# A sparse attention with two feed-forward stages: the product with v in 64x64 tiles, its halves added in DRAM, the last keys' transposes in spare PSUM columns

## The chip, the cores and the metric

One core of one Trainium2 chip runs the whole program. The metric is the device time of one execution in microseconds; the core is the only one, so it is also the slowest. TensorE, VectorE, ScalarE, GpSimd and SyncE run side by side, each through its own instructions in order; TensorE accumulates in PSUM, eight banks of 512 float32 columns on 128 partitions, and DMA queues move data to and from DRAM.

## The reference, cut to what matters

```python
def _attn_ref(q, k, v, tau):             # (4, 8, 576, 64) each
    scores = scale * np.matmul(q, k.transpose(0, 1, 3, 2))
    thresh = np.max(scores, axis=-1, keepdims=True) - tau
    scores = np.where(scores >= thresh, scores, -1000000000.0)
    attn = np.exp(scores - np.max(scores, axis=-1, keepdims=True))
    attn = attn / (np.sum(attn, axis=-1, keepdims=True) + 1e-09)
    return np.matmul(attn, v)

x = attn_out.transpose(0, 2, 1, 3).reshape(2304, 512)
x = ((x @ w_a) * (x @ w_b)) @ w_out      # 512 -> 1536 -> 512
h = x @ w_in                             # 512 -> 1024
solu = h * softmax(h)
out = layernorm(solu) * g_ln @ w_out     # 1024 -> 512
```

All arrays are float32. The change touches the first part, attention, alone.

## The kernel before, in words

**Pairs and steps.** The 32 heads are handled as 16 pairs of two heads (index `i` or `j`). A pair has 576 queries and keys a head; they are cut into nine score blocks (`NS` = 9, index `s`): blocks 0 to 7 are 128 queries of one head, block 8 the last 64 queries of both heads. The loop over `m` takes two blocks a step, "A" and "B", so 72 steps hold the scores of all pairs and six more steps drain what follows. Two pairs take nine steps, so the work of step `m` repeats with `m` mod 9. `PROG` lists, by letters, the order in which a step emits its parts, and that order is each engine's order.

**One step.** `scores` (A, B) multiplies q and k in four 64x64 tiles of the array into a two-bank PSUM tile `ps`, 288 of the 512 columns of each bank; the pool has two such tiles, one for A and one for B. `soft_max` (VectorE, line 692) negates and scales them into SBUF and takes the row minimum; `soft_exp` (ScalarE, line 704) takes the exponentials; `soft_thr` (t, u; GpSimd, line 709) makes the threshold; `soft_mask` (a, b; VectorE, line 718) applies it and sums the row. One step later `tpose` (T, U; line 738) transposes the masked blocks on TensorE into a PSUM tile `tp`, four 128-column transposes a block, and ScalarE copies them to SBUF (line 731). The 64 last keys of two blocks (`tq`, line 754) and those of block 8 (line 757, a product with the identity) go through `tpose_tail` (Y) into another tile of the same three-buffer pool.

**The product with v.** `pv` (V; line 769) has one accumulation for 256 queries (`r` = 1) and one for 320 queries and two columns of ones (`r` = 2): 128 keys a product for `kc` 0 to 3, two heads in the two column halves of the array (128x64 tiles), and for `kc` = 4 the last 64 keys of the two heads, with zeros in the other head's rows of `vz`. The dictionary `PV` spreads these over the steps: pair `j` begins at step `j*9//2 + 4`, two or three `kc` a step. ScalarE then copies `po` to `xp` (line 777), and SP stores `xp` to the DRAM tensor `xd` in the next step (line 779). `finish` (F) transposes the reciprocal row sums and stores them to `rzd`.

**Beside it.** In steps 6 to 41 `conv_emit` slips in the preparation of the next stage's weights in a fixed order: at most one VectorE operation in `fill` (letter f, ahead of the masks) and up to three ScalarE or GpSimd operations at the step's end. GpSimd's are tensor_tensor operations of 256 or 512 elements (line 237), and `gate` makes them wait for the step's last mask. At step 46 the program loads `rzd` and `xd` of the first third of the tokens (`load_z(0)`, `load_x(0)`), and from step 51 a list `STEPS` hands out their normalisation and splitting, at steps 65 and 66 `load_z(1)` and `load_x(1)`; from step 69 VectorE normalises the second third (line 483). After the loop `load_x(2)` loads the last third (line 470), and the second stage, `moe1`, begins; its weight loads `wraw` (line 200) follow on SP's queue, which works in order. `bank["y"]` are four PSUM tiles that take the place of the score tiles from step 72.

Of the kernel before, what the change touches and what calls it, by code (L numbers as in the profile page):

```python
# [21 lines left out]
def kernel(  # L22
# [607 lines left out]
    def attention():  # L630
        es, es_r = ExitStack(), ExitStack()
        slots, late, bulk = [], [], []
        conv_ops = conv_first()
        ps_a = es.enter_context(tc.tile_pool(name="ps_a", bufs=3, space=PSUM))
# [10 lines left out]
        dt = {}  # L645
        for k in (0, 1, "t"):
            for r in (1, 2):
                shape = [P] + ([] if k == "t" else [NQ]) + [R1 if r == 1 else R2 + 2]
                dt[k, r] = d = pt.tile(shape, F32, name=f"pt{k}{r}")
                if r == 2:  # L650
                    nc.vector.memset(d[(slice(None),) * (len(shape) - 1) + (slice(R2, R2 + 2),)], 1.0)
        vz = [pt.tile([P, 2, D], F32, name=f"vz{k}") for k in range(3)]
        for z in vz:
            nc.gpsimd.memset(z, 0.0)
# [78 lines left out]
        def tpose(i, s):  # L733
            pe = st[i, s]
# [11 lines left out]

        def tpose_tail(i, s):
            pe = st.pop((i, s))
            if s == 3 or s == 2 * NQ:
                r, q0, n = (1, 0, R1) if s == 3 else (2, 2, R2)  # L750
# [9 lines left out]
        def pv(i, r, half):  # L760
            n = R1 if r == 1 else R2 + 2
            if half == 0:
                st[i, "o", r] = ps_a.tile([P, 512], F32, name="po", bufs=1)
            po = st[i, "o", r][:, 0:n]
            vr, vt = ld[i, "v"], vz[i % 3]

            def mm(kc, h):
                lhsT, rhs = (vr[:, h * NQ + kc], dt[h, r][:, kc, 0:n]) if kc < NQ else (vt[:, h], dt["t", r][:, 0:n])
                nc.tensor.matmul(po[h * D:(h + 1) * D], lhsT=lhsT, rhs=rhs, start=(kc == 0), stop=(kc == NQ), skip_group_check=True)  # L769

            def store():
                b, hp = divmod(i, NPAIR)
                if r == 1:
                    st[i, "x"] = px.tile([P, S + 2], F32, name="xp")
# [6 lines left out]
            if half == 1:  # L781
                pv_q.append(store)
            cut = NQ // 2
            return [lambda kc=kc, h=h: mm(kc, h) for kc in (range(cut) if half == 0 else range(cut, NQ + 1)) for h in range(2)]

        def finish(i):
            b, hp = divmod(i, NPAIR)
            rz = st.pop((i, "rz"))
            t1 = ps_a.tile([P, 512], F32, name="rt1", tag="tp")
            nc.tensor.transpose(t1[0:NS, 0:P], rz, ident)  # L790
            zt = sm.tile([NS, P], F32, name="zt", bufs=2)
            zd = rzd[b][2 * hp:2 * hp + 2]

            def store():
                nc.scalar.activation(out=zt, in_=t1[0:NS, 0:P], func=AF.Copy)
# [5 lines left out]
        PV = [{x: (k // 2 + 1, k % 2) for k, x in enumerate(d)} for d in ([4, 5, 6, 7], [4, 5, 7, 8])]  # L801
# [41 lines left out]
        PROG = 'ABtuVFTUYXfab'  # L843
# [5 lines left out]
        for m in range(tot // 2 + 6):  # L849
# [43 lines left out]
            for ch in PROG:  # L893
                if ch in "AB":
                    score("AB".index(ch))
                elif ch == "V":
                    for mm in mms:
                        mm()
                elif ch == "F":
                    for j in range(NP):  # L900
                        if m - j * NS // 2 == 8:
                            finish(j)
                elif ch in "TU":
                    turn("TU".index(ch))
                elif ch == "Y":
                    for c in old:
                        tpose_tail(*c)
# [27 lines left out]
            bulk.clear()  # L935
            for fn in dma_q + later:
# [17 lines left out]
            if m in conv_at:  # L954
                conv_emit("AP", 3)
# [15 lines left out]
        for fn in dma_q + later:  # L971
# [526 lines left out]
```

## Time and profile before

| | us |
|---|---|
| median of 3 runs | 902.83 |
| lowest and highest of them | 902.67 and 903.42 |
| the profiled execution | 902.6 |
| its span, first to last instruction | 900.8 |
| steps 9 to 71 of attention, in the profile | from 35.73 to about 264 |

The profiled execution's own time is 1.8 us more than its span, and 0.2 us under the median. TensorE's granted clock is full in the whole span. A busy TensorE is not one at its peak, so the starts of its weight loads are read below, and waits are read where the engine in question sat idle.

### The profile page before, as it was taken

How to read it: one execution, taken by the hardware profiler on the slowest of the kernel's cores; microseconds unless marked ns; L12 is line 12 of the kernel's file. 1: busy time of each engine (PE TensorE's matmuls, PEld its weight loads, DVE VectorE, ACT ScalarE, POOL GpSimd, SP SyncE). 2: the span in 40 equal slices, each digit the busy share in tenths (PEclk: the TensorE clock that was granted, in tenths of full speed). 3: DMA queues.
4: the chain of work that ended last, by engine and by line, in shares of the span. 5: the costliest groups of instructions: out<-in, count | busy, mean ns of one | idle time of the engine just before them, and what ended most of it. 6: DMA issues, size and time to landing. Idle time of an engine off the chain costs nothing.

```text
span 900.8 us, 16285 instructions
## 1 busy us (share of the span) xinstructions
PE 881.3 (98%) x5842; PEld 732.7 (81%) x5842; DVE 690.3 (77%) x1508; ACT 530.3 (59%) x1010; POOL 161.7 (18%) x296
## 2 busy tenths in 40 slices
PE   7999999999989999999999999999999999999998
PEld 3555555555558899999999999999999778888886
DVE  6989988899988877876586655775544898888873
ACT  5888877878965465554454444544445465555543
POOL 1143321124412010002121121211113000000000
PEclk9999999999999999999999999999999999999999
DMA  6435334566555869489965998588869011110001
GB/s 176 155 112 150 117 106 126 133 175 212 167 188 175 252 241 313 139 313 314 354 117 115 317 337 230 104 216 268 255 138 213 25 43 52 47 47 24 24 25 47
DMA packets 71280, 147.71 MB, mean 164 GB/s; under 512 B 11040, under 2 KB 41376, under 8 KB 71200
## 3 DMA queue, kind: packets, MB, share of 16 engines
q1 hardware_dynamic: 60032, 131.84, 43.7%
q0 software_dynamic: 10368, 14.16, 10.8%
q8 instruction: 46, 0.75, 0.3%
q10 hardware_dynamic: 800, 0.68, 0.3%
q14 instruction: 34, 0.28, 0.1%
HBM read 98.06 MB, written 48.59 MB: 163 GB/s over the span
## 4 chain that ended last, share of the span: by engine, by line
PE 82%; DVE 9%; issue 3%; ACT 2%; DMA 2%; POOL 1%; ACTq 0%; SPq 0%; DVEq 0%; POOLq 0%
PE acc L611 28%; PE py L1098 16%; PE po L1392 10%; PE ph L1271 9%; PE po L769 5%; PE ps L687 5%; PE tp L738 5%; DVE pe L718 3%; DVE ns L692 3%; PE pl L1369 2%; POOL st_t L237 1%; PE py L611 1%; ACT pe L704 1%; DMA rzd<-zt 1%; DMA q<-in_qkv_dram 1%
## 5 line engine op out<-in xcount | busy, mean ns | idle before, releaser
L611 PE MATMUL acc<-xt,w 128*128 128x384 f32 x1446 | 270.6, 336 | 2.6 <-DVE xt L237 2.6
L611 PEld LDWEIGHTS acc<-xt,w 128*128 128x128 f32 x1446 | 254.4, 188 | 3.6 <-DVE xt L237 3.6
L704 ACT ACTIVATE pe<-ns,nm 128x576 f32<-128x576 f32 x128 | 94.0, 775 | 47.7 <-DVE ns L692 47.0
L1076 POOL DMA_DIRECT2D yd<-y x68 | 59.0, 891 | 305.2 <-ACT y L1072 209.4
L692 DVE TENSOR_SCALAR_CACHE_REDUCE ns<-ps 128x576 f32<-128x576 f32 x144 | 103.1, 752 | 8.9 <-PE ps L687 8.6
L718 DVE SCALAR_TENSOR_TENSOR pe<-ns,th,pe 128x576 f32<-128x576 f32 x128 | 100.2, 813 | 6.2 <-ACT pe L704 3.8
L1392 PE MATMUL po<-w,lt 128*128 128x512 f32 x432 | 103.5, 395 | 0.0
L687 PE MATMUL ps<-k,q 64*64 64x288 f32 x1152 | 90.1, 424 | 5.2 <-DMA k<-in_qkv_dram 3.6
L1392 PEld LDWEIGHTS po<-w,lt 128*128 128x128 f32 x432 | 79.8, 188 | 16.8
L1072 ACT ACTIVATE y<-py 128x384 f32<-128x384 f32 x92 | 45.0, 490 | 75.9 <-PE py L1098 73.9
L1098 PE MATMUL py<-ga,wo 128*128 128x384 f32 x432 | 84.0, 334 | 0.0
L1098 PE MATMUL py<-gb,wo 128*128 128x384 f32 x432 | 84.0, 334 | 0.0
L769 PE MATMUL po<-pt,vr 128*64 128x322 f32 (+1 forms) x512 | 77.6, 419 | 1.5 <-ACT pt L731 1.1
L731 ACT ACTIVATE pt<-tp 128x512 f32<-128x512 f32 (+1 forms) x160 | 77.9, 544 | 1.6 <-PE tp L738 0.8
L738 PEld LDWEIGHTS tp<-ident,pe 128*128 128x128 f32 x512 | 56.5, 143 | 26.0 <-issue 9.9
L709 POOL TENSOR_SCALAR th<-nm,toff 128x1 f32<-128x1 f32 x144 | 47.4, 331 | 158.7 <-DVE ns L692 153.1
L1098 PEld LDWEIGHTS py<-ga,wo 128*128 128x128 f32 x432 | 75.7, 188 | 0.0
L1098 PEld LDWEIGHTS py<-gb,wo 128*128 128x128 f32 x432 | 75.7, 188 | 0.0
L1271 PE MATMUL ph<-w,ys 128*128 128x512 f32 x297 | 74.5, 393 | 0.7 <-ACT h L1275 0.7
L738 PE MATMUL tp<-ident,pe 128*128 128x128 f32 x512 | 71.8, 280 | 2.4 <-DVE pe L718 1.2
L1271 PEld LDWEIGHTS ph<-w,ys 128*128 128x128 f32 x297 | 55.6, 188 | 13.7 <-ACT h L1275 1.1
L769 PEld LDWEIGHTS po<-pt,vr 128*64 128x64 f32 x512 | 32.0, 136 | 42.5 <-issue 17.1
(148 smaller groups left out, 1186.5 us busy)
## 6 DMA issues: line engine op xcount, KB each, us to landing
xt<-opd SPq DMA_DIRECT2D x42, 768.0 KB
wraw<-in_w_dram SPq DMA_DIRECT2D x36, 512.0 KB
opd<-xt SPq DMA_DIRECT2D x21, 768.0 KB
yd<-y POOLq DMA_DIRECT2D x68, 192.0 KB, 5.3
q<-in_qkv_dram SPq DMA_DIRECT2D x15, 576.0 KB
k<-in_qkv_dram SPq DMA_DIRECT2D x30, 176.0 KB
xd<-xp SPq DMA_DIRECT2D x16, 289.0 KB
yd<-y SPq DMA_DIRECT2D x24, 192.0 KB
```

The costliest lines, as they stand in the source:

```text
L611: nc.tensor.matmul(ps, lhsT=w[:, WOP[j], wi, c * P:(c + 1) * P], rhs=x[:, c, xi, :], start=(k == 0 and j < 3), stop=(k == 3 * QK - 1 and j ...
L687: nc.tensor.matmul(ps[t * D:(t + 1) * D, g, 0:HS], lhsT=q[r, u, c], rhs=k[r, u, o:o + HS], start=True, stop=True, skip_group_check=True)
L692: nc.vector.tensor_scalar(out=ns, in0=st[i, s][:, :, 0:HS], scalar1=-SCALE, scalar2=None, op0=ALU.mult, op1=ALU.min, accum_out=nm)
L704: nc.scalar.activation(out=pe.rearrange("p (g s) -> p g s", g=2), in_=ns, func=AF.Exp, bias=nm, scale=-1.0)
L718: last_mask[0] = nc.vector.scalar_tensor_tensor(out=pv, in0=ns, scalar=th, in1=pv, op0=ALU.is_le, op1=ALU.mult, accum_out=z[:, s:s + 1])
L731: evac_q.append(lambda: nc.scalar.activation(out=out, in_=in_, func=AF.Copy))
L738: nc.tensor.transpose(tp[:, kc, :], pe[:, o:o + P], ident)
L769: nc.tensor.matmul(po[h * D:(h + 1) * D], lhsT=lhsT, rhs=rhs, start=(kc == 0), stop=(kc == NQ), skip_group_check=True)
L1076: nc.gpsimd.dma_start(out=to[:, g["oc"], :], in_=y, accum_op=ALU.add)
L1098: nc.tensor.matmul(g["py"], lhsT=wos[g["q"] * F1 + r][:, wi, oc * P:(oc + 1) * P], rhs=g["g"][r][:, gi, :], start=(r == c == 0), stop=last ...
L1271: nc.tensor.matmul(ps, lhsT=v[:, a, c * P:(c + 1) * P], rhs=w[:, b], start=(k == 0 and j < 3), stop=(k == 3 * QK - 1 and j in (2, 4, 6)), ...
L1392: nc.tensor.matmul(po, lhsT=lt[:, a, j, :], rhs=w2(j, b), start=(k == 0), stop=(k == 3 * NJ - 1))
```

## The change

`pv` works in 64x64 tiles: each product over 128 keys becomes two over 64 keys, in the two row halves of the array, and each row half has a PSUM bank of its own. `po` takes two banks and its pool `tp` has two buffers in place of three. The last keys need no zeros, so `vz` with its fills and loads goes. ScalarE copies both banks to `xp`, SP stores the first half, and GpSimd adds the second half to it in DRAM by an accumulating DMA, two steps after the copy was emitted. `load_x` reads what was added up. The products of `PV` are spread anew. The last keys' transposes, and that of the row sums, go to the columns of the A block's score tile that hold no scores (from step 72 into `bank["y"][3]`); block 8's, in 64x64 tiles, directly behind the product with v (`tail_end`). They are copied out by ScalarE at the new letter E, that is behind the step's two exponentials. `conv_emit` emits at most some 512 elements of GpSimd's operations a step.

```diff
-        ps_a = es.enter_context(tc.tile_pool(name="ps_a", bufs=3, space=PSUM))
+        ps_a = es.enter_context(tc.tile_pool(name="ps_a", bufs=2, space=PSUM))
-        vz = [pt.tile([P, 2, D], F32, name=f"vz{k}") for k in range(3)]
-        for z in vz:
-            nc.gpsimd.memset(z, 0.0)
...
-            vr = pv_p.tile([P, VS - 1, D], F32, name="vr")
-            nc.sync.dma_start(out=vr, in_=v[i, :, 0:VS - 1])
-            for h in range(2):
-                hh = slice(h * D, (h + 1) * D)
-                nc.sync.dma_start(out=vz[i % 3][hh, h], in_=v[i, hh, VS - 1])
+            vr = pv_p.tile([P, VS, D], F32, name="vr")
+            nc.sync.dma_start(out=vr, in_=v[i])
...
             ps = ps_s.tile([P, 2, 512], F32, name="ps")
+            if (i * NS + s) % 2 == 0:
+                side["ps"] = ps
...
+        def spare(c0, width):
+            if "y" in bank:
+                return bank["y"][3].rearrange("p (k c) -> p k c", k=2)[:, :, c0:c0 + width]
+            return side["ps"][:, :, HS + c0:HS + c0 + width]
+
+        def tail_end(i, s):
+            if s < 2 * NQ:
+                return
+            te = spare(P, D)
+            for h in range(2):
+                rows = slice(h * D, (h + 1) * D)
+                to, part, by = (te[rows, 0], slice(None), ident[:, rows]) if "y" in bank else (te[rows, h], rows, ident[rows, rows])
+                nc.tensor.matmul(to, lhsT=st[i, s][part, SM:S], rhs=by, start=True, stop=True, skip_group_check=True)
+                if "y" not in bank:
+                    evac(dt["t", 2][rows, R1:R2], te[rows, h])
+            if "y" in bank:
+                evac(dt["t", 2][:, R1:R2], te[:, 0])
...
-                tq = ps_a.tile([P, 512], F32, name="tq", tag="tp")
+                tq = spare(0, P)
...
-                    nc.tensor.transpose(tq[:, u * P:(u + 1) * P], pa.rearrange("p h s -> p (h s)")[:, SM:SM + P], ident)
-                if r == 2:
-                    for h in range(2):
-                        nc.tensor.matmul(tq[h * D:(h + 1) * D, R1:R2], lhsT=pe[:, SM:S], rhs=ident[:, h * D:(h + 1) * D], start=True, stop=True)
-                evac(dt["t", r][:, 0:n], tq[:, 0:n])
+                    nc.tensor.transpose(tq[:, u], pa.rearrange("p h s -> p (h s)")[:, SM:SM + P], ident)
+                evac(dt["t", r][:, 0:R1].rearrange("p (u c) -> p u c", u=2), tq)
...
+            def mm(kc, h, g):
+                rows = slice(g * D, (g + 1) * D)
+                if kc < NQ:
+                    lhsT, rhs = vr[rows, h * NQ + kc], dt[h, r][rows, kc, 0:n]
+                elif g == h:
+                    lhsT, rhs = vr[rows, 2 * NQ], dt["t", r][rows, 0:n]
+                else:
+                    return
+                nc.tensor.matmul(po[h * D:(h + 1) * D, g], lhsT=lhsT, rhs=rhs, start=(kc == 0), stop=(kc == NQ - (g != h)), skip_group_check=True)
...
-                nc.scalar.activation(out=xp[:, c0:c0 + n], in_=po, func=AF.Copy)
+                nc.scalar.activation(out=xp[:, :, c0:c0 + n], in_=po, func=AF.Copy)
                 if r == 2:
-                    dma_q.append(lambda: nc.sync.dma_start(out=xd[b][:, hp, :], in_=xp))
+                    dma_q.append(lambda: nc.sync.dma_start(out=xd[b][:, hp, :], in_=xp[:, 0]))
+                    adds.append((m + 2, lambda: nc.gpsimd.dma_start(out=xd[b][:, hp, :], in_=xp[:, 1], accum_op=ALU.add)))
...
-            t1 = ps_a.tile([P, 512], F32, name="rt1", tag="tp")
+            t1 = spare(0, P)[0:NS, 1]
...
-        PV = [{x: (k // 2 + 1, k % 2) for k, x in enumerate(d)} for d in ([4, 5, 6, 7], [4, 5, 7, 8])]
+        PV = ({4: (1, 0, 3), 5: (1, 3, 5), 6: (2, 0, 2), 7: (2, 2, 5)}, {4: (1, 0, 2), 5: (1, 2, 4), 6: (1, 4, 5), 7: (2, 0, 3), 8: (2, 3, 5)})
...
-        def conv_emit(engs, count=1):
+        def conv_emit(engs, count=1, most=0):
             while conv_ops and count and conv_ops[0][0] in engs + "S":
+                if most and conv_ops[0][0] == "P":
+                    if conv_ops[0][1] > most:
+                        return
+                    most -= conv_ops[0][1] - 1
...
-        PROG = 'ABtuVFTUYXfab'
+        PROG = 'ABtuVFYETUXfab'
...
                     for mm in mms:
                         mm()
+                    for c in old:
+                        tail_end(*c)
...
+                elif ch == "E":
+                    for fn in evac_q:
+                        fn()
+                    evac_q = []
...
+            while adds and adds[0][0] <= m:
+                dma_q.append(adds.pop(0)[1])
             for fn in dma_q + later:
...
-                conv_emit("AP", 3)
+                conv_emit("AP", 3, 515)
...
-        for fn in dma_q + later:
+        for fn in dma_q + [fn for _, fn in adds] + later:
             fn()
         later.clear()
         load_x(2)
```

## Rows read from the trace of the kernel before

**Rows 1.** Section 4 of the page: shares of the chain, by line.

```profile
PE acc L611 28%; PE py L1098 16%; PE po L1392 10%; PE ph L1271 9%; PE po L769 5%; PE ps L687 5%; PE tp L738 5%; DVE pe L718 3%; DVE ns L692 3%; PE pl L1369 2%; POOL st_t L237 1%; PE py L611 1%; ACT pe L704 1%; DMA rzd<-zt 1%; DMA q<-in_qkv_dram 1%
```

**Rows 2.** Windows: length, each engine's busy us, clock, DMA share, GB/s.

```profile
35.73:133.79 98.06, 96.99 (x943) 56.76 (x943) 88.30 (x247) 80.76 (x158) 35.67 (x71) 1.00 0.42 129
133.79:165.65 31.86, 31.86 (x315) 18.74 (x315) 27.23 (x79) 25.18 (x49) 4.77 (x18) 1.00 0.33 99
197.51:230.43 32.92, 32.32 (x316) 18.64 (x315) 32.25 (x89) 28.76 (x56) 14.41 (x26) 1.00 0.56 182
```

**Rows 3.** Timeline, TensorE's weight loads of steps 45 and 46: start, us, instructions.

```profile
165.65 0.69 PEld L687 LDWEIGHTS ps<-k,q 64*64 64x64 f32 x16 [0.17 <-issue]
166.78 0.63 PEld L769 LDWEIGHTS po<-pt,vr 128*64 128x64 f32 x8 [0.44 <-issue]
168.23 0.42 PEld L738 LDWEIGHTS tp<-ident,pe 128*128 128x128 f32 x4 [0.39 <-ACT pe L704]
169.73 0.69 PEld L687 LDWEIGHTS ps<-k,q 64*64 64x64 f32 x16
170.86 0.86 PEld L738 LDWEIGHTS tp<-ident,pe 128*128 128x128 f32 x8 [0.44 <-ACT ptt L731]
171.89 0.69 PEld L687 LDWEIGHTS ps<-k,q 64*64 64x64 f32 x16 [0.16 <-issue]
```

**Rows 4.** Timeline, step 42, from its scores to its masks.

```profile
154.88 0.69 PEld L687 LDWEIGHTS ps<-k,q 64*64 64x64 f32 x16
156.47 1.46 ACT L704 ACTIVATE pe<-ns,nm 128x576 f32<-128x576 f32 x2 [0.86 <-DVE ns L692]
157.34 0.82 DVE L718 SCALAR_TENSOR_TENSOR pe<-ns,th,pe 128x576 f32<-128x576 f32 x1 [0.23 <-ACT pe L704]
```

**Rows 5.** Groups by form, 0 to 380 us: ScalarE's copies out of PSUM.

```profile
L731 ACT ACTIVATE pt<-tp 128x512 f32<-128x512 f32 x128 | 69.1, 584 | 1.4 <-PE tp L738 0.8
L731 ACT ACTIVATE ptt<-tq 128x256 f32<-128x256 f32 x16 | 6.2, 388 | 0.0
L777 ACT ACTIVATE xp<-po 128x322 f32<-128x322 f32 x16 | 6.7, 421 | 4.3 <-PE po L769 4.3
```

**Rows 6.** Timeline, GpSimd and VectorE about step 31.

```profile
117.74 1.54 POOL L237 TENSOR_TENSOR st_t<-st_a,st_t 128x256 f32<-128x256 f32 x2
119.55 0.82 DVE L718 SCALAR_TENSOR_TENSOR pet<-ns,th,pet 128x576 f32<-128x576 f32 x1 [1.90 <-POOL th L709]
```

**Rows 7.** Timeline, 239 to 262 us, SP's queue and VectorE.

```profile
239.81 2.61 SPq L454 DMA_DIRECT2D sc<-rzd  x4
250.48 1.26 SPq L779 DMA_DIRECT2D xd<-xp  x1
258.07 0.81 DVE L718 SCALAR_TENSOR_TENSOR pe<-ns,th,pe 128x576 f32<-128x576 f32 x1
```

**Rows 8.** Window at that stretch's end, columns as in rows 2.

```profile
258.00:259.00 1.00, 0.05 (x1) 0.05 (x1) 1.00 (x4) 0.00 (x0) 0.00 (x0) 1.00 0.32 99
```

**Rows 9.** Page section 5 and the source view of line 1076.

```profile
L1076 POOL DMA_DIRECT2D yd<-y x68 | 59.0, 891 | 305.2 <-ACT y L1072 209.4
...
DMA to landing us min/median/max: 3.5/5.7/10.3
```

**Rows 10.** Timeline, from the last scores into the second stage.

```profile
268.62 3.07 PEld L611 LDWEIGHTS py<-xt,w 128*128 128x128 f32 x18
271.95 1.83 PEld L769 LDWEIGHTS po<-pt,vr 128*64 128x64 f32 x16 [0.25 <-issue]
275.40 0.32 SPq L779 DMA_DIRECT2D xd<-xp  x1
277.21 1.24 SPq L470 DMA_DIRECT2D x<-xd  x2
279.99 0.52 SPq L200 DMA_DIRECT2D wraw<-in_w_dram  x1
290.13 0.66 ACT L216 ACTIVATE st_a<-wraw 128x512 f32<-128x512 f32 x1
```

More of the change, by code (lines that the diff above doesn't have):

```diff
@@ L631, in attention @@
         es, es_r = ExitStack(), ExitStack()
-        slots, late, bulk = [], [], []
+        slots, late, bulk, adds = [], [], [], []
         conv_ops = conv_first()
-        ps_a = es.enter_context(tc.tile_pool(name="ps_a", bufs=3, space=PSUM))
+        ps_a = es.enter_context(tc.tile_pool(name="ps_a", bufs=2, space=PSUM))
         px = es.enter_context(tc.tile_pool(name="px", bufs=2))
@@ L645, in attention @@
         dt = {}
+        side = {}
         for k in (0, 1, "t"):
@@ L733, in tpose @@
         def tpose(i, s):
-            pe = st[i, s]
+            pe = st.pop((i, s))
             tp = ps_a.tile([P, NQ, P], F32, name="tp")
@@ L747, in tpose_tail @@
         def tpose_tail(i, s):
-            pe = st.pop((i, s))
             if s == 3 or s == 2 * NQ:
-                r, q0, n = (1, 0, R1) if s == 3 else (2, 2, R2)
-                tq = ps_a.tile([P, 512], F32, name="tq", tag="tp")
+                r, q0 = (1, 0) if s == 3 else (2, 2)
+                tq = spare(0, P)
                 for u in range(2):
                     pa = st.pop((i, "p", q0 + u))
-                    nc.tensor.transpose(tq[:, u * P:(u + 1) * P], pa.rearrange("p h s -> p (h s)")[:, SM:SM + P], ident)
-                if r == 2:
-                    for h in range(2):
-                        nc.tensor.matmul(tq[h * D:(h + 1) * D, R1:R2], lhsT=pe[:, SM:S], rhs=ident[:, h * D:(h + 1) * D], start=True, stop=True)
-                evac(dt["t", r][:, 0:n], tq[:, 0:n])
@@ L760, in pv @@
-        def pv(i, r, half):
-            n = R1 if r == 1 else R2 + 2
[L762 to L769, printed above, removed]
+                    nc.tensor.transpose(tq[:, u], pa.rearrange("p h s -> p (h s)")[:, SM:SM + P], ident)
@@ new lines, in tpose_tail, with pv @@
+                evac(dt["t", r][:, 0:R1].rearrange("p (u c) -> p u c", u=2), tq)
+        def pv(i, r, ka, kz):
+            n = R1 if r == 1 else R2 + 2
+            if ka == 0:
+                st[i, "o", r] = ps_a.tile([P, 2, 512], F32, name="po", bufs=1)
+            po = st[i, "o", r][:, :, 0:n]
+            vr = ld[i, "v"]
+            def mm(kc, h, g):
[7 more added lines that the diff above has]
+                nc.tensor.matmul(po[h * D:(h + 1) * D, g], lhsT=lhsT, rhs=rhs, start=(kc == 0), stop=(kc == NQ - (g != h)), skip_group_check=True)
@@ L773, in store @@
                 if r == 1:
-                    st[i, "x"] = px.tile([P, S + 2], F32, name="xp")
+                    st[i, "x"] = px.tile([P, 2, S + 2], F32, name="xp")
                 xp = st[i, "x"]
                 c0 = 0 if r == 1 else R1
-                nc.scalar.activation(out=xp[:, c0:c0 + n], in_=po, func=AF.Copy)
+                nc.scalar.activation(out=xp[:, :, c0:c0 + n], in_=po, func=AF.Copy)
                 if r == 2:
-                    dma_q.append(lambda: nc.sync.dma_start(out=xd[b][:, hp, :], in_=xp))
-            if half == 1:
+                    dma_q.append(lambda: nc.sync.dma_start(out=xd[b][:, hp, :], in_=xp[:, 0]))
+                    adds.append((m + 2, lambda: nc.gpsimd.dma_start(out=xd[b][:, hp, :], in_=xp[:, 1], accum_op=ALU.add)))
+            if kz == NQ + 1:
                 pv_q.append(store)
-            cut = NQ // 2
-            return [lambda kc=kc, h=h: mm(kc, h) for kc in (range(cut) if half == 0 else range(cut, NQ + 1)) for h in range(2)]
+            return [lambda kc=kc, h=h, g=g: mm(kc, h, g) for kc in range(ka, kz) for g in range(2) for h in range(2)]
         def finish(i):
@@ L788, in finish @@
             rz = st.pop((i, "rz"))
-            t1 = ps_a.tile([P, 512], F32, name="rt1", tag="tp")
-            nc.tensor.transpose(t1[0:NS, 0:P], rz, ident)
+            t1 = spare(0, P)[0:NS, 1]
+            nc.tensor.transpose(t1, rz, ident)
             zt = sm.tile([NS, P], F32, name="zt", bufs=2)
             zd = rzd[b][2 * hp:2 * hp + 2]
+            evac(zt, t1)
             def store():
-                nc.scalar.activation(out=zt, in_=t1[0:NS, 0:P], func=AF.Copy)
                 dma_q.append(lambda: nc.sync.dma_start(out=zd[:, 0:SM].rearrange("h (c q) -> c h q", q=P), in_=zt[0:2 * NQ]))
@@ L906, in attention @@
                     for c in old:
-                        tpose_tail(*c)
+                        if c[1] == 3 or c[1] == 2 * NQ:
+                            tpose_tail(*c)
                 elif ch in "tu":
```

## The prediction, made before the change was built

> **What bounds the kernel now.** I read the chain of waits first [rows 1]. It runs through TensorE for most of the span; attention's part of it are lines 769, 687 and 738. The reader is to see that VectorE's masks and scalings are in it too, with 3% each, and one GpSimd line with 1%: attention is held by TensorE, but nothing is far behind.
>
> Then the windows of nine steps [rows 2]. 31.86 us is a period without the next stage's preparation; TensorE is busy in all of it, VectorE in 27.23. With the preparation, three periods take 98.06, 2.5 more than three times 31.86. With the loading of the second stage's operands VectorE is busy 32.25 of 32.92 and sets the pace.
>
> Last, the starts of TensorE's weight loads [rows 3], because they show what a period is made of. A float32 product is two instructions, and tiles that don't overlap run side by side, so scores are four rounds of 288 columns (sixteen loads, four at a time), the product with v in step 45 six rounds of 256 (two at a time), the transposes of step 46 eight rounds of 128. From scores to what follows it is 1.13 us, from that product to the transposes 1.45: (1.45 - 1.13) / (1536 - 1152 columns) = 0.833 ns a column, and 1.13 - 0.96 = 0.17 is left, which I take as the price of going from one shape of tile to another. The transposes bear it out: 0.85 + 0.17 = 1.02 against 1.03. A period before is then 9 x (0.96 + 0.85) for scores and transposes, 9.63 for the products with v (20 rounds of 256 columns and 20 of 322), 1.15 for last keys and row sums, and 28 switches (three in six steps, four in the two with block 8's keys, two in the one without a product) of 0.17: 31.83, against 31.86 measured. So TensorE waits for nobody in such a period, and a saved switch is a saved 0.17.
>
> **The product with v in quarter tiles** has the same number of rounds: half the rows, twice as many tiles side by side. What goes is the switch between scores and product, in eight of nine steps, and with block 8's last keys moved in behind the product, that of line 757 in two steps: 28 switches become 18, 1.70 us a period. The trace of before has quarter tiles only in the scores; they run four at a time there, so I take the same here.
>
> **The last keys in the score tile** bring a wait. The next step's A scores need that tile, so they wait until ScalarE has copied the last keys out, and those copies stand behind the step's two exponentials, which end 3.05 us after the step's first load (156.47 + 1.46 - 154.88) [rows 4]. A copy of 256 columns takes 0.39 [rows 5], two small ones ahead of it some 0.14 each: in steps 0 and 5 (mod 9) the tile is free after about 3.70. TensorE's own work there is 0.96 + 0.85 + 0.11 + 0.17 + 0.21 + 0.85 + 0.17 = 3.32, so it waits 0.37, twice. Step 8, 3.05 long, waits about 0.2 for the row sums; step 2, behind the short step 1, about 0.1; step 6 about 0.2 for `po`, which is copied later and over twice the columns (512 take 0.58, before 322 took 0.42 [rows 5]). That is 1.3 of the 1.7, and 0.4 a period is left. Bounds: all of 1.7 if VectorE and ScalarE run ahead, nothing if they come 0.2 later.
>
> **The limit on GpSimd.** Three operations in one step (512, 256, 256 elements) hold up the next threshold: the last two end at 119.28 and the mask behind them waited 1.90 [rows 6]; three such places make up the 2.5 of the windows. At most one large one goes now, 1.3 us, which fits under scaling and exponential. But VectorE's part of the preparation is then spread over more steps, and each such operation, ahead of the masks, makes the next exponentials and so the last keys' copies late. I take 1.6 of the 2.5: with 3 x 0.4 the steps 9 to 35 gain 2.8 (bounds 1 and 5).
>
> **From step 36 to 65.** 0.4 for the next period. In the one after, the load at step 46 keeps SP's queue full, pair 9's store lands late, and the add behind it on GpSimd holds a threshold: I take 0.5 lost. In steps 54 to 65 VectorE has no slack [rows 2], and its delays go through the exponentials into the wait on the tile: 0.9 lost. Sum to step 65: 1.8 gained (bounds -0.5 and 4.5).
>
> **The adds.** Sixteen accumulating DMAs go onto GpSimd's queue, ahead of the next step's thresholds, which the masks wait for; each waits until the store of the first half has landed. GpSimd is busy 4.8 of 31.9 us [rows 2], in a step it is free for over 2 us at a stretch, and an issue takes 0.89 [rows 9], so most cost nothing. Pair 13's does. At the end of step 65 SP issues the row sums' load (239.81), then operands and `xd` loads, and that pair's store at 250.48, at the back of a full queue that runs dry only within the window from 258 [rows 7, 8]: landed about 258.9, 19.1 after the first load. Behind it come a delay to the waiting engine (0 to 1, I take 0.5), 0.89 for the issue, 0.3 for the threshold, 0.1: the mask of step 69 can start 20.9 after that load. Before it started at 258.07, 18.3 after [rows 7]. That is 2.6 lost, and the few tenths that steps 66 to 68 gain are lost in it. At step 69 the kernel is 0.8 behind (bounds -2 and 3).
>
> The 68 issues of the second stage took 0.89 in the mean beside a busy VectorE [rows 9], and that is what I use. The Trainium skill, in "SBUF — State Buffer", section "SBUF: two separate sides", warns against just this kind of move: a DMA from GpSimd cannot get its descriptors written while VectorE runs an instruction that takes both SBUF ports. By its figures, 0.62 us alone and 3.1 beside such instructions, the sixteen adds would cost some tens of microseconds (an estimate).
>
> **Behind the last scores.** In step 72 block 8's last keys stand ahead of the transposes, which so wait for the last mask: 0.3. The products of `PV` for pair 15 end their first accumulation in step 73, behind the eighteen products of the second stage (268.62 to 271.95 [rows 10]) and not ahead of them: a switch (0.17) and two rounds of 256 (0.43). Then `po` must be copied before the second accumulation starts: 0.3 until the copy begins, 0.59 for it [rows 5], 0.05. Before, that accumulation followed the eighteen at once. 1.8 lost, and nothing covers it; 2.6 with the 0.8.
>
> **The hand-over.** The store of pair 15 (275.40) comes 2.6 + 0.25 later; it has landed 1.8 after its issue, since the load of `xd` was issued then (277.21) [rows 10]. Now the add comes between: from its issue 3.5 to 10.3 us to landing, median 5.7 [rows 9]; on a quiet queue I take 4.5. The load then goes at 284.5 and not 277.2, 7.3 later, 4.7 more than the rest of the program is. Behind it on SP stand `wraw` loads, the first issued at 279.99 before, and ScalarE needs that one at 290.13 [rows 10]. It stood behind 2.3 MB and may have landed by 288, so 2.1 are free; 2.6 are a stall of ScalarE, on which the second stage's PSUM tiles wait. With gaps of ScalarE that take up 0.6 I take 2.0 (bounds 0 and 7). "DMA: Bandwidth & Descriptors" of the Trainium skill, section "Anatomy of one DMA — SWDGE (gpsimd) path", gives 2.0 us and the bytes over 436 GB/s, here 2.7 us (an estimate); by it the stall would nearly vanish and the time be some 1.8 lower. No landing in this trace was as short.
>
> **The sum.** -1.8 + 2.6 + 1.8 + 2.0 = +4.6 us. Against the profiled execution's 902.6 that is 907.2; the median of the runs stands 0.2 above that execution, which I don't correct for.
>
> **The rivals.** First, **faster: the tile comes free in time.** Place: the next A scores; price: up to 1.3 us a period over seven and a half periods, 9.6. For it: VectorE is idle for 4.6 us of a period [rows 2]. Against it: ScalarE can't begin the copies before its exponentials end, whatever VectorE's slack. With the whole 9.6 the time is 897.6; it falls below 901 once the waits come to less than 0.45 a period.
>
> Second, **the two queue waits are hidden**: pair 13's store lands earlier because its queue starts earlier, or the last load's delay meets a free `wraw`. Each takes 2.0 to 2.6 away: 904.6, or 902.6 without both. Against it: both follow the queue's order, and the first is bound to loads that start with the same step of the loop.
>
> Third, **GpSimd's adds cost every time**: an issue longer than the free stretch of 2 us holds the thresholds up at each of sixteen pairs; at 1 us each 16 more, 923. It decides from an issue of some 2 us. Against it stands the mean of 68.
>
> Fourth, **the quarter tiles don't run four at a time**: the 9.6 us of rounds a period double, 72 us more, 979. Against it: the scores.
>
> **How the numbers follow.** Forecast, slower by 2 to 10 us: 0.52. Hidden queue waits, 902.6 to 904.6: 0.24. Faster: 0.17. Adds every time: 0.04. Quarter tiles: 0.03. A measurement of this kernel tells about 0.2%, 1.8 us, from no change. Below 901.0 is the faster rival; from 901.0 to 904.6 the second and a little of the first; above it the rest. The range leaves out most of the faster rival and the two dear ones: 900.5 to 912.5. The forecast's own runs from 904.6 to 912.5, by the bounds of the landing and of the gain to step 65.
>
> **What would show it.** Steps 0 and 5 near 3.7 us, with TensorE's scores waiting for ScalarE's line 731; no gap of weight loads between scores and product; a wait of the masks of step 69 on GpSimd, and of GpSimd on a DMA; SP's load of `xd` 6 to 8 us behind the last store, then ScalarE waiting for `wraw`. The prediction is wrong if a nine-step period without preparation falls to 31 or below, or if the second stage's first units keep the distance to the end of attention that they have now.

## The result, and the profile after

The changed kernel takes 913.44 us (median of 5 runs, 912.02 to 914.38), the kernel before 902.67 beside it: ratio 1.0116, 95% interval [1.0102, 1.0131]. It is slower, as predicted, but by 10.8 us and not by 4.6. The profiled execution took 912.2, its span is 910.4; it is 1.3 us faster than the median of its kernel, so what is read in this one trace adds up to 9.6 us and not to 10.8.

Section 4 of the page, the shares of the chain, against [rows 1]:

```profile
PE 80%; DVE 7%; DMA 4%; ACT 4%; issue 2%; SPq 1%; POOL 0%; ACTq 0%; POOLq 0%; DVEq 0%
PE acc L611 26%; PE py L1130 16%; PE po L1424 10%; PE ph L1303 9%; PE po L787 6%; PE ps L684 5%; PE tp L735 5%; DVE pe L715 2%; DVE ns L689 2%; DMA xd<-xp 2%; PE pl L1401 2%; DMA xt<-opd 1%; ACT pe L701 1%; DMA wraw<-in_w_dram 1%; PE ps L769 1%
```

A DMA of `xp` to `xd` stands in the chain with 2% (somebody waits for a store or an add), a load of `wraw` with 1%; neither stands in [rows 1]. The first place to look is there. But first the windows, for the same steps as [rows 2] (9 to 35, 36 to 44, 54 to 62):

```profile
37.04:131.84 94.80, 94.30 (x1135) 59.13 (x1134) 88.72 (x245) 85.76 (x170) 40.29 (x75) 1.00 0.53 152
131.84:162.98 31.14, 31.09 (x379) 19.84 (x379) 27.56 (x77) 26.61 (x53) 7.84 (x22) 1.00 0.44 121
195.24:228.57 33.33, 31.97 (x380) 19.43 (x379) 32.25 (x89) 29.67 (x58) 15.92 (x28) 1.00 0.64 192
```

Steps 9 to 35 take 94.80 instead of 98.06, a period without preparation 31.14 instead of 31.86: attention itself became faster. With the second stage's operands (the last row) it is 33.33 instead of 32.92. The weight loads of steps 36 and 37 (timeline) show how, beside [rows 3]:

```profile
131.84 0.69 PEld L684 LDWEIGHTS ps<-k,q 64*64 64x64 f32 x16 [0.17 <-issue]
132.62 0.83 PEld L787 LDWEIGHTS po<-pt,vr 64*64 64x64 f32 x16
...
135.19 0.21 PEld L684 LDWEIGHTS ps<-k,q 64*64 64x64 f32 x8 [0.17 <-issue]
135.77 0.21 PEld L684 LDWEIGHTS ps<-k,q 64*64 64x64 f32 x8 [0.37 <-ACT ptt L728]
```

The product's loads follow the scores' at once (132.62 - 131.84 = 0.78, with no idle time; 1.13 before): that switch of tile shape is gone. In step 37 the second tile's scores wait 0.37 for ScalarE's copies of the last keys.

Then step 69 (timeline; SP, VectorE, GpSimd and TensorE), against [rows 7]:

```profile
238.30 2.61 SPq L454 DMA_DIRECT2D sc<-rzd  x4
249.90 0.39 SPq L797 DMA_DIRECT2D xd<-xp  x1
255.57 0.23 DVE L480 TENSOR_SCALAR vs<-vs,neg 128x8 f32<-128x8 f32 x1 [3.92 <-DMA vs<-xd]
258.60 0.89 POOL L798 DMA_DIRECT2D xd<-xp  x1 [9.87 <-DMA xd<-xp]
259.27 0.77 POOL L706 TENSOR_SCALAR th<-nm,toff 128x1 f32<-128x1 f32 x2
259.85 0.82 DVE L715 SCALAR_TENSOR_TENSOR pe<-ns,th,pe 128x576 f32<-128x576 f32 x1 [3.00 <-POOL th L706]
262.14 0.29 PEld L769 LDWEIGHTS ps<-ident,pe 128*128 128x128 f32 x2 [6.68 <-DVE ns L689]
262.42 1.72 PEld L735 LDWEIGHTS tp<-ident,pe 128*128 128x128 f32 x8
```

Read the brackets from the top: GpSimd stood idle for 9.87 us, until the store of 249.90 had landed and it could issue pair 13's add. The thresholds stand behind the add; VectorE waited 3.00 for them before the mask, and TensorE 6.68 for the scaling that follows the masks. Its eight transposes' loads then take 1.72, where eight took 0.86 in [rows 3]. The windows (granted clock is the third number from the end) say why:

```profile
256.00:258.00 2.00, 0.04 (x2) 0.00 (x0) 0.85 (x2) 0.00 (x0) 0.00 (x0) 1.00 0.47 183
258.00:260.00 2.00, 0.00 (x0) 0.00 (x0) 0.15 (x1) 0.00 (x0) 1.40 (x3) 0.88 0.01 3
260.00:262.00 2.00, 0.00 (x0) 0.00 (x0) 2.00 (x5) 0.00 (x0) 0.04 (x1) 0.50 1.03 145
262.00:264.00 2.00, 1.85 (x9) 1.85 (x10) 2.00 (x7) 1.87 (x4) 0.76 (x2) 0.50 0.03 3
```

Last the hand-over from attention to the second stage (timeline), against [rows 10]:

```profile
276.11 1.84 PEld L787 LDWEIGHTS po<-pt,vr 64*64 64x64 f32 x32 [1.15 <-ACT xp L795]
...
280.18 0.33 SPq L797 DMA_DIRECT2D xd<-xp  x1
281.95 6.41 SPq L470 DMA_DIRECT2D x<-xd  x2
282.82 0.88 POOL L798 DMA_DIRECT2D xd<-xp  x1 [0.78 <-DMA xd<-xp]
290.36 0.83 SPq L200 DMA_DIRECT2D wraw<-in_w_dram  x2
298.36 0.66 ACT L216 ACTIVATE st_a<-wraw 128x512 f32<-128x512 f32 x1 [3.44 <-DMA wraw<-in_w_dram]
300.59 5.82 PEld L611 LDWEIGHTS acc<-xt,w 128*128 128x128 f32 x25 [3.04 <-ACT c L1218]
```

The two loads of `xd` take SP 6.41 where they took 1.24, since the second waits for the add; `wraw` leaves 10.4 later than before, is there 8.0 after that, and ScalarE waits 3.44 for it, TensorE 3.04 for ScalarE. The window behind it has 0.83 of the clock:

```profile
300.00:310.00 10.00, 8.07 (x36) 7.71 (x37) 7.19 (x14) 6.28 (x12) 0.00 (x0) 0.83 0.30 105
```

As a ledger, in us against the kernel before, for this kernel and those below that take it apart: starts of scores (steps 9 to 69), then of VectorE's first scaling in step 71, then of VectorE's multiplication in the first and fourth unit of the second stage; the time behind that changes by at most 0.5. VectorE's rows (timeline), before and then changed:

```profile
263.46 0.75 DVE L692 TENSOR_SCALAR_CACHE_REDUCE ns<-ps 128x576 f32<-128x576 f32 x1
280.29 0.55 DVE L1190 TENSOR_TENSOR c<-c,c 128x384 f32<-128x384 f32 x1
304.44 0.56 DVE L1190 TENSOR_TENSOR c<-c,c 128x384 f32<-128x384 f32 x1
...
265.78 0.76 DVE L689 TENSOR_SCALAR_CACHE_REDUCE ns<-ps 128x576 f32<-128x576 f32 x1 [0.47 <-PE ps L684]
284.96 0.55 DVE L1222 TENSOR_TENSOR c<-c,c 128x384 f32<-128x384 f32 x1
313.60 0.56 DVE L1222 TENSOR_TENSOR c<-c,c 128x384 f32<-128x384 f32 x1
```

| kernel (profiled execution) | step 9 | step 36 | step 45 | step 69 | step 71 | unit 1 | unit 4 |
|---|---|---|---|---|---|---|---|
| changed | +1.3 | -2.0 | -2.7 | -2.1 | +2.3 | +4.7 | +9.2 |
| e8: before, with the limit on GpSimd | +0.4 | -2.1 | -2.1 | -2.1 | -2.5 | -2.5 | -2.5 |
| e6: changed, half tiles, no adds | +1.5 | -0.1 | +0.2 | +1.2 | +1.1 | +3.2 | +3.2 |
| e3: changed, adds left out | +1.3 | -2.0 | -2.7 | -3.1 | -2.9 | -0.7 | -0.7 |
| e1: changed, pair 13's add later | +1.1 | -2.1 | -2.8 | -2.5 | -1.0 | +1.2 | +7.4 |
| e2: changed, another order in step 70 | +0.5 | -2.7 | -3.4 | -2.6 | +1.2 | +4.4 | +10.4 |
| e7: changed, TensorE kept busy in step 70 | +0.2 | -3.0 | -3.8 | -3.0 | +0.6 | +2.8 | +9.3 |
| e5a: changed, pair 15 without add | +0.5 | -2.8 | -3.5 | -3.0 | +1.2 | +3.3 | +3.3 |
| e11: changed, load behind `wraw` | +0.5 | -2.7 | -3.4 | -2.5 | +1.9 | +4.1 | +5.9 |

Each row is one execution. Steps 0 to 8 differ by up to 1.1 from one to another, in kernels that are the same there. The hand-over, from unit 1 to unit 4, is the same in e1, e2 and e7 as in the changed kernel; it took 4.5 in the one and 6.1 to 6.5 in the other three, so a difference of a us or two in a single trace is not yet an effect.

### The profile page after: what moved, and what is told of

Its sections match the earlier page's. It is cut to its first block, busy times and chain, and to the rows that moved or that the text cites. A ratio compares the mean times of both kernels' runs of the same rounds, so it can differ in the third digit from the quotient of the medians.

```text
span 910.4 us, 17279 instructions
## 1 busy us (share of the span) xinstructions
PE 880.8 (97%) x6354; PEld 742.6 (82%) x6354; DVE 692.0 (76%) x1508; ACT 542.4 (60%) x1041; POOL 175.0 (19%) x309
## 3 DMA queue, kind: packets, MB, share of 16 engines
HBM read 98.06 MB, written 53.32 MB: 166 GB/s over the span
## 4 chain that ended last, share of the span: by engine, by line
PE 80%; DVE 7%; DMA 4%; ACT 4%; issue 2%; SPq 1%; POOL 0%; ACTq 0%; POOLq 0%; DVEq 0%
PE acc L611 26%; PE py L1130 16%; PE po L1424 10%; PE ph L1303 9%; PE po L787 6%; PE ps L684 5%; PE tp L735 5%; DVE pe L715 2%; DVE ns L689 2%; DMA xd<-xp 2%; PE pl L1401 2%; DMA xt<-opd 1%; ACT pe L701 1%; DMA wraw<-in_w_dram 1%; PE ps L769 1%
## 5 line engine op out<-in xcount | busy, mean ns | idle before, releaser
L684 PE MATMUL ps<-k,q 64*64 64x288 f32 x1152 | 93.6, 431 | 5.1 <-DMA k<-in_qkv_dram 3.3
L787 PE MATMUL po<-pt,vr 64*64 64x322 f32 (+1 forms) x1024 | 77.2, 407 | 2.1 <-ACT xp L795 1.6
L706 POOL TENSOR_SCALAR th<-nm,toff 128x1 f32<-128x1 f32 x144 | 49.4, 353 | 127.7 <-DVE ns L689 123.5
L735 PEld LDWEIGHTS tp<-ident,pe 128*128 128x128 f32 x512 | 58.7, 144 | 11.0 <-issue 5.5
L684 PEld LDWEIGHTS ps<-k,q 64*64 64x64 f32 x1152 | 36.3, 136 | 37.5 <-issue 8.4
```

Source lines behind the costliest of these rows:

```text
L735: nc.tensor.transpose(tp[:, kc, :], pe[:, o:o + P], ident)
L787: nc.tensor.matmul(po[h * D:(h + 1) * D, g], lhsT=lhsT, rhs=rhs, start=(kc == 0), stop=(kc == NQ - (g != h)), skip_group_check=True)
```

## The experiments

All times are medians of several runs; each ratio is to the kernel before, run beside it, with its 95% interval.

**e3, without the adds.** The line that appends to `adds` is removed.

```
-  adds.append((m + 2, lambda: nc.gpsimd.dma_start(out=xd[b][:, hp, :], in_=xp[:, 1], accum_op=ALU.add)))
```

> All sixteen adds are left out, so the product's second half-sums are missing from what the second stage reads. If the two waits behind adds (step 69, the hand-over) are what the change costs: step 70 takes 5.7 us, the load of batch 3 goes out within 3 us of the last store, and the time falls by 9 to 11 us, to 902.5 to 904.5, level with the kernel before. If the cost lies in the product and the last keys themselves (the tail behind the last scores, the start): it falls by 6 us or less and stays above 907.

901.86, 0.9989 [0.998, 0.9998], a little below the expected range. The adds are the whole loss, 11.5 us by the ratios (1.0116 - 0.9989); everything else together gains 1.

**e1, pair 13's add a step later.**

```
-  adds.append((m + 2, ...
+  adds.append((m + 2 + (i == 13), ...
```

> Pair 13's add is put on GpSimd one step later, behind the thresholds of step 69 and not ahead of them. Theory (that add, waiting for its store, holds up the thresholds, TensorE runs dry and then works at half clock): the mask of step 69 starts near 256.5 and not at 259.85, step 70 takes 5.7 and not 11.3 us, the windows from 260 to 266 show a granted clock of 1.00, and the time falls by 5 to 6 us, to about 908. Rival (VectorE waits at 255.57 for the row sums' load anyway, and the last keys, now ahead of the transposes, are what TensorE waits for): the mask moves by 1 to 2 us, the clock still falls, and the time falls by 2 us or less, to 911 or above.

910.27, 1.0074 [1.0062, 1.0087]: 3.2 to 3.8 us less, between the two. Its timeline of VectorE and its windows:

```profile
256.59 0.81 DVE L715 SCALAR_TENSOR_TENSOR pe<-ns,th,pe 128x576 f32<-128x576 f32 x1
...
258.00:260.00 2.00, 1.11 (x6) 1.12 (x7) 2.00 (x8) 1.14 (x2) 1.57 (x3) 0.75 0.25 17
260.00:262.00 2.00, 2.00 (x14) 1.35 (x16) 2.00 (x6) 2.00 (x5) 0.68 (x2) 0.50 0.85 125
```

The mask starts where the theory had it, but TensorE is still idle for 3.25 us, until 258.9 (VectorE waits for the load of `vs` first), and the clock still falls. In the trace unit 1 starts 3.5 earlier than in the changed kernel's (+1.2) and unit 4 only 1.7 (+7.4). The medians don't bear out that the hand-over takes half of the gain back: they are 3.2 apart. Pair 15's add moved with the end of attention (issued at 279.28 and not 282.82), so the wait behind it stays.

**e2, last keys behind the transposes in step 70 alone.**

```
+  for ch in 'ABtuVFTUYEXfab' if m == 70 else PROG:
```

> In step 70 alone, the last keys' transposes stand behind the two tiles' transposes again, as in the kernel before. If the wait of GpSimd is the cause and the order only adds the wait for one more scaling: the first transposes start 1 to 1.5 us earlier, the clock still falls, and the time falls by 0.5 to 1.5 us, to about 912.5. If the order is the cause: step 70 takes 7 us or less, the clock stays at 1.00, and the time falls by 4 to 5 us.

912.77, 1.0101 [1.0083, 1.0119]: 0.7 to 1.4 less, with intervals that overlap, and the clock falls all the same. The order is not the cause.

**e4, pair 15's halves added by VectorE.**

```
+  nc.vector.tensor_tensor(out=xp[:, 0], in0=xp[:, 0], in1=xp[:, 1], op=ALU.add)   # i == 15, no add in DRAM
```

> Pair 15's two half-sums are added by VectorE before its store, and its add in DRAM is gone; the other fifteen adds stay. If the hand-over costs what its load is late by: the load of batch 3 goes out some 4 us earlier, ScalarE waits for the weights' first load by under 1 us and not 3.44, the clock holds at 300 to 310, and the time falls by 3.5 to 5 us, to about 909. If the stall is mostly hidden (the prediction's 2.0, or less): it falls by 1 to 2 us.

913.41, 1.0114 [1.01, 1.0128]: nothing. The experiment brought a stall of its own, as VectorE's timeline shows: it stands 8.99 us behind ScalarE's last copy, with the second stage's preparation queued behind it. It tells nothing of the hand-over.

```profile
280.08 0.76 DVE L798 TENSOR_TENSOR xp<-xp 128x578 f32<-128x578 f32 x1 [8.99 <-ACT xp L795]
```

**e5a and e5b, pair 15, then pairs 13 and 15, in half tiles**, so that they need no add.

```
+  def whole(kc, h):
+      rows = slice(h * D, (h + 1) * D)
+      lhsT, rhs = (vr[:, h * NQ + kc], dt[h, r][:, kc, 0:n]) if kc < NQ else (vr[rows, 2 * NQ], dt["t", r][rows, 0:n])
+      nc.tensor.matmul(po[rows, 0], lhsT=lhsT, rhs=rhs, start=(kc == 0), stop=(kc == NQ), skip_group_check=True)
```

> Pair 15 alone has its product with v in half tiles again (128 rows), so that it has no second half-sum and no add, and nothing is put on VectorE for it. If the late load at the hand-over costs 4.6 us: wraw's load is issued near 284 as in the kernel before (shifted by what attention is late), ScalarE's line 216 doesn't wait for it, the granted clock holds between 290 and 310, and the time falls by 4 to 5 us, to about 908.5. If most of the delay is hidden: it falls by less than 2 us.

> Pairs 13 and 15 have their products in half tiles, so neither has an add; the other fourteen keep quarter tiles and adds. If these two adds are the whole price of the change: 902 to 903.5, the level of the kernel with all adds left out plus 0.6 for pair 9's add. If the other adds cost as well, or the return of the switches in ten steps does: 905 or more.

e5a: 907.2, 1.0044 [1.0031, 1.0058], 6.2 to 6.5 less and so more than expected; e5b: 903.9, 1.001 [1.0002, 1.0019], between its two expectations. In e5a the second stage keeps its distance to attention (+3.3 in both units); `wraw` leaves at 283.33 and ScalarE doesn't wait (timelines of SP and ScalarE):

```profile
283.33 4.27 SPq L200 DMA_DIRECT2D wraw<-in_w_dram  x2
293.44 0.67 ACT L216 ACTIVATE st_a<-wraw 128x512 f32<-128x512 f32 x1
```

With both gone 9.6 of the 11.5 us are back (1.0116 - 1.001): two adds of sixteen are most of the price, pair 15's some 6.3 and pair 13's some 3.2.

**e11, the load behind `wraw`.** All adds stay; `load_x(2)` leaves batch 3's part to the second load of `wraw` behind attention.

```
+  if p == 2 and b == 3 and not force:
+      pend.append(lambda: load_x(2, True))
+      continue
```

> The changed kernel with all its adds; only the load of batch 3, which waits for pair 15's add, stands on SP's queue behind the two loads of wraw and not ahead of them. If the hand-over costs what wraw is late by: wraw's load is issued near 283, ScalarE's line 216 doesn't wait, the clock holds from 290 to 310, and the time falls by 4 to 5 us, to about 908.5. If it is the operands of batch 3 themselves that come late, or the add's traffic: within 1 us of 913.

908.57, 1.0062 [1.0048, 1.0076], as the theory had it, and the clock is 1.00 from 290 to 310. So most of what pair 15's add costs, 4.9 of some 6.3, is not that its data come late, but what stands behind the waiting load on SP. In the trace 1.9 us are still lost between units 1 and 4; in them ScalarE waits once. The timeline names a load of `wraw`:

```profile
290.00 0.63 ACT L248 ACTIVATE wo<-st_a 128x512 fp32r<-128x512 f32 x1 [3.06 <-DMA wraw<-in_w_dram]
```

A wait for several semaphores is put down to the one that came last by the profile, and here it was another. The chain of work, followed back over the semaphores, goes from this instruction to the add of pair 15:

```profile
279.53 2.13 DMA xd<-xp
...
282.18 4.77 DMA xd<-xp
286.95 2.98 issue
...
290.00 0.63 ACT wo L248
```

The add, issued at 282.18, lands at 289.86, and ScalarE starts 0.14 later. In e12, e13 and e14 the same instruction starts 0.15 behind the landing of that add, in the changed kernel too (287.65 and 287.80, where it cost 0.23), and in e3 and e5a, without the add, it waits for nothing. It is the first that writes `wo`, whose pool is opened behind attention; probably it takes memory that held `xp`, which the add reads, but no run shows that. So pair 15's add has two engines waiting for it, SP and ScalarE, and e11 frees the first alone.

**e6, half tiles for all pairs, no adds; e8, the kernel before with the limit alone.** e6 is the edit of e5a for every pair. e8:

```
-  conv_emit("AP", 3)
+  conv_emit("AP", 3, 515)   # and conv_emit's "most", as in the change
```

> All products with v in half tiles and no adds at all; the last keys' transposes in spare columns, the limit on GpSimd and the order of the steps stay as changed. It is set against the kernel with the adds left out (901.9). If a switch of tile shape costs 0.17 us and TensorE sets the pace: a nine-step period without preparation takes 0.4 to 1.3 us more than the 31.1 of the changed kernel, and the time is 3 to 9 us above 901.9. If the switch costs nothing, or the waits on scalings and copies set the pace: the period stays within 0.2 of 31.1 and the time within 1.5 of 901.9.

> The kernel before with nothing but the limit on GpSimd's preparation. If the drops of 1.4 to 1.55 us that the changed kernel shows at steps 14, 23 and 32 are the limit's alone: they stand here too, step 36 begins 4 to 5 us earlier than before, and the time falls by 4 us or more, to 898.5 (less where the load at step 46 or the row sums' load at 65 hold it up again). By the prediction's 1.6: 901. If the limit only moves work to where it costs as much: within 1 us of 903.

e6: 905.14, 1.0026 [1.0016, 1.0036]. e8: 900.19, 0.9969 [0.9957, 0.998], the fastest of all kernels here. Windows of steps 9 to 35 and 36 to 44, e8, then e6, then e3:

```profile
36.09:131.67 95.58, 95.58 (x943) 56.27 (x942) 88.99 (x247) 81.73 (x158) 34.11 (x69) 1.00 0.44 132
131.67:163.53 31.86, 31.86 (x315) 18.76 (x314) 27.46 (x79) 25.18 (x49) 6.18 (x20) 1.00 0.33 99
```

```profile
37.22:133.70 96.48, 96.48 (x943) 55.60 (x943) 89.13 (x247) 83.86 (x170) 35.74 (x69) 1.00 0.42 130
133.70:165.84 32.14, 32.14 (x315) 18.57 (x314) 27.63 (x79) 25.83 (x53) 6.18 (x20) 1.00 0.32 99
```

```profile
37.02:131.84 94.82, 94.32 (x1135) 59.13 (x1134) 88.74 (x245) 85.90 (x170) 35.09 (x69) 1.00 0.43 133
131.84:162.99 31.15, 31.10 (x380) 19.82 (x379) 27.57 (x77) 26.62 (x53) 6.18 (x20) 1.00 0.34 102
```

The limit gives 2.5 us in steps 9 to 35 (98.06 to 95.58) and nothing elsewhere, as it should. From e8 to e6 (last keys in the score tile, the new order and split) a period loses 0.28. That need not be a price of the last keys' new place: by the order of the loads e6 has 30 switches a period and not 28, since its edit puts the last keys' product in 64x64 tiles behind products of 128x64 (its timeline; idle time in front):

```profile
145.91 0.19 PEld L792 LDWEIGHTS po<-ptt,vr 64*64 64x64 f32 x4 [0.49 <-issue]
```

Two switches at the prediction's 0.17 make 0.34. From e6 to e3 (quarter tiles, 18 switches) a period gains 0.99; twelve switches of 0.17 would make 2.04, so about half of that must be lost again in waits, such as the 0.37 of step 37.

**e7 and e13, TensorE kept busy in step 70**, in the changed kernel and in e11.

```
+  if ch == "V" and m == 70:
+      dummy = ps_a.tile([P, NQ, P], F32, name="tp")
+      for _ in range(6):
+          nc.tensor.matmul(dummy.rearrange("p a b -> p (a b)"), lhsT=ident, rhs=ld[15][0][:, 0, 0:512], start=True, stop=True)
```

> Six products of 512 columns (0.85 us each by the rows of the product with v), whose result nobody reads, stand behind the scores of step 70, in the stretch from 256 to 262 in which TensorE has nothing to do. If the half clock behind that stretch costs time of its own: the windows from 262 to 267 show 1.00, the transposes of step 70 take 0.86 and not 1.72, the scores of step 71 1.2 and not 2.1, and the time falls by 1.5 to 2.5 us. If VectorE sets the pace there: the clock holds and the time stays within 0.7 us.

> The same with the add where the change has it, and the six products nobody reads that keep TensorE at its full clock through the idle stretch of step 70. If the half clock behind that stretch is the greater part of the stall's price: 906.5 or less. If the mask's 1.8 us is the greater part, and the half clock costs some 0.8 on its own: 907.3 to 908.2.

e7: 912.61, 1.0104 [1.0091, 1.0118]. e13: 908.73, 1.0064 [1.005, 1.0077], against 1.0062 for e11 and above both of its expected ranges. The clock is held, as this window of e13 shows, and the time falls by 0.8 to 1.1 (e7, with intervals that overlap) or not at all (e13):

```profile
262.00:264.00 2.00, 1.95 (x22) 1.48 (x26) 2.00 (x5) 1.97 (x4) 0.76 (x2) 1.00 0.03 5
```

VectorE is busy through that window, as it is without the products: it, more than TensorE's clock, sets the pace behind a late mask. From the mask of step 69 to VectorE's first scaling of step 71 it takes 5.93 in the changed kernel (259.85 to 265.78), 5.39 in e13 and 5.39 in the kernel before (258.07 to 263.46), so the half clock costs some 0.5 there.

**e12, e11 with pair 13's add later (e1's edit).**

> The changed kernel with the hand-over's load behind wraw's (908.6 alone) and pair 13's add one step later. Theory: the stall at step 69 costs 3.5 us at the end of attention, of which the hand-over hid a part when it was mended alone; with wraw's load in time the whole shows: 904.5 to 905.5. Rival: something else takes the time up behind it: 907 or more.

905.6, 1.0028 [1.0017, 1.004], 3.0 under e11, just above the expected range. e1 against the changed kernel gave 3.2: moving pair 13's add is worth about 3 with the late load and without it, so the medians show nothing that the hand-over had hidden.

**e9 and e10, the tail.** e9 is e5b with pair 15's product split as before, and its row sums' transpose in a tile of `ps_a`; e10 puts pair 9 in half tiles too. e14 is e12 with the edit of e9.

```
+  PV15 = {4: (1, 0, 2), 5: (1, 2, 5), 7: (2, 0, 3), 8: (2, 3, 5)}   # for pair 15
+  t1 = ps_a.tile([P, NQ, P], F32, name="tp")[0:NS, 0] if "y" in bank else spare(0, P)[0:NS, 1]
```

> Set against the kernel with pairs 13 and 15 in half tiles (903.9): pair 15's first accumulation ends ahead of the second stage's eighteen products again, and its row sums' transpose goes to a tile of attention's own and not to the second stage's bank. If the tail behind the last scores costs what the prediction took, 1.8: the time falls by 1.5 to 2.5 us, to about 902. If the end of attention is hidden behind the loads of the hand-over: within 0.7 us of 903.9.

> The last one with pair 9 in half tiles as well, so that its add (behind a store that the load at step 46 makes late) is gone. If that add costs the 1.1 us that the kernel without adds doesn't lose at step 52: another 0.5 to 1 us less, about 901.2. If only the switches come back: 0.3 us more.

> All quarter tiles and all sixteen adds kept, with three changes of order alone: the load behind wraw's, pair 13's add a step later, pair 15's product and row sums as before. 1 to 2 us under the first of these three, about 903.5, level with the kernel before and 3 above the kernel with only the limit.

e9: 902.78, 0.9994 [0.9985, 1.0003]; e10: 901.75, 0.9983 [0.9975, 0.9992]; e14: 904.0, 1.0015 [1.0006, 1.0024]. Each step is 1.0 to 1.6 us, in the direction expected, but the intervals of neighbours touch or overlap, so the sizes are rough.

## Why the prediction was right in direction and wrong in size

**To step 69: right, by other parts, and so in part by luck.** Forecast -1.8 at step 65; the trace says -1.8 there and -2.1 at step 69. The limit was taken at 1.6 and is 2.5, all that the windows of [rows 2] had offered; it needed no discount. A period without preparation gains 0.72, forecast 0.4 of 1.7: the waits on the last keys' copies are there with the size forecast (0.37; 0.30 in step 42), though the second tile's scores wait, not the first's, and steps 36 and 41 take 3.35 and not 3.7. Against these gains stands a loss in the first nine steps that was not foreseen. Part of it, 0.6, is in step 6 (4.04 for 3.42; e8 has 3.42), where the second tile's scores wait 0.53 for the last keys' copies and the product 0.56 for ScalarE, which copies `po` (line 795) in between; the step was taken at 0.2. Pair 9's add cost 1.1 and not 0.5 (step 54: -2.3, in e3 -3.3).

**Pair 13's add: mechanism right, 2.6 forecast, 3.3 in the trace.** GpSimd behind the DMA, the mask behind GpSimd, each as described. From the row sums' load to the mask it is 21.55 (238.30 to 259.85), forecast 20.9, before 18.26; the add starts 20.3 after that load and not 19.6. The medians say 3.0 to 3.8 (e12 against e11, e1). That TensorE would fall to half its clock was not foreseen; in e7 and e13, which hold it, the time is not clearly lower.

**Behind the last scores: 1.8 forecast, 2.2 to 2.4.** From step 71 (+2.3) to unit 1 (+4.7) of the changed kernel it is 2.4; in e3, from -2.9 to -0.7, 2.2. A wait of 0.55 for the row sums' copy out of the second stage's bank had been missed.

**The hand-over: the step that failed, 2.0 forecast, 4.5 in this trace and some 6 in others.** The chain was the one forecast (load behind the add, `wraw` behind the load, ScalarE behind `wraw`; e11 shows it by changing the order alone), its price was mis-sized in three places.

First, from store to load it took 7.6 (280.18 to 281.95 + 6.41 - 0.55 = 287.81) and not 6.3. Of this the store's landing is 2.6 and not 1.8 (the add leaves at 282.82), and the add 5.0 from its issue to the load, not 4.5. The 1.8 was a misreading of [rows 10]: the row of 277.21 stands for two loads, the first of them is batch 2's, and pair 15 belongs to batch 3, whose load is the second, 2.5 behind the store (timeline of the kernel before, from 277.8 on):

```profile
277.88 0.57 SPq L470 DMA_DIRECT2D x<-xd  x1
```

That 2.1 us were free for `wraw` was right: it took 8.0 from issue to use, and by that it was there at 288.0 before (an estimate). Second, I let ScalarE's gaps take up 0.6 of the stall. They took up nothing: ScalarE waited 3.44 where 2.6 were forecast, TensorE 3.04 for ScalarE and then ran at 0.83 of its clock, and 4.5 were lost by unit 4. Third, a landing is no fixed time: in the traces of e1, e2 and e7, with the same hand-over, the add took 5.0 to 5.6 from issue to landing (4.8 in the changed kernel's) and `wraw` 8.4 to 9.0, and 6.1 to 6.5 were lost. By medians pair 15's add costs 6.2 to 6.5 (e5a). With this term at its upper bound of 7 and the rest as forecast the time would have been 912.2; the small misses of the others carried it above that.

The Trainium skill, "DMA: Bandwidth & Descriptors", section "Anatomy of one DMA — SWDGE (gpsimd) path", would have made the landing 2.7 (an estimate from its figures). The measured adds, which run beside the program's other transfers, disagree; the source view of line 798:

```profile
L798 POOL DMA_DIRECT2D xd<-xp x16: 855/887/1085, 40.5 to 282.8; - x16
...
DMA to landing us min/median/max: 4.1/5.4/8.1
```

The same rows bear on the rule of the Trainium skill's "SBUF — State Buffer", section "SBUF: two separate sides": no issue took over 1.09, with VectorE busy for most of attention; whether one of VectorE's instructions beside them took both ports the trace doesn't say.

**The sum.** In the trace: -2.1 at step 69, +4.4 to step 71 (of which 3 are given back when the add moves), +2.4, +4.5, and 0.4 later: 9.6. Forecast -1.8, 2.6, 1.8, 2.0. The medians are 10.8 apart; the 1.2 that this trace doesn't hold are of the size by which its hand-over is shorter than the others', but no trace of a longer execution of this kernel shows that.

**The rivals.** That the tile comes free in time didn't happen, but the "wrong if" bound was close: 31.14 where 31 was named. The hidden queue waits didn't happen; both waits are in the trace. Adds that cost every time: e5b, with fourteen of them, stands 2 us above e3 with none, not 14. The quarter tiles do run four at a time (sixteen loads in 0.83, and no period doubled).

## What to carry to other kernels

An accumulating DMA costs little itself (0.89 us on GpSimd), but it waits in order behind its store, and what waits for it (here SP's load of the sum and ScalarE's first write of `wo`) holds up all that stands behind on its own queue: before moving a sum to DRAM, list for each queue what stands behind both waits, and at the end of a stage put the loads of the next stage ahead. When a change has several parts, time its smallest one alone: here the few lines that keep three GpSimd operations out of one step (e8) were worth 2.9 us, and the rest of the change cost 13.

## What the runs showed of the hardware that was not expected

In the stretch from 256 to 262 us, in which TensorE had nothing to do, its granted clock went from 1.00 to 0.50 (from 2.4 to 1.2 GHz), and eight weight loads of 128x128 behind it took 1.72 instead of 0.86. In e13, with six products in that stretch, it stayed at 1.00, and the time was that of e11.

One hand-over, the same in four kernels, took 4.5, 6.1, 6.3 and 6.5 us in their traces. e1's trace alone says that half of what moving pair 13's add gains is taken back behind attention (unit 1: 3.5 earlier, unit 4: 1.7); the medians, 3.2 here and 3.0 where the load no longer stands in the way (e12 against e11), say that nothing is. A price that hangs on the landing of a DMA is read from several executions.
